# Feed-forward products by Strassen's algorithm, with streamed weights, behind an attention and Fourier kernel

## The chip, the cores and the metric

The kernel runs on one core of a Trainium2 chip. The metric is the device time of one execution in microseconds (us). Engines are named as the profile names them: PE is TensorE (PEld its weight loads), DVE is VectorE, ACT is ScalarE, POOL is GpSimd, SP is SyncE, which only issues DMAs; POOL issues DMAs too.

## The reference

```python
scores = np.matmul(q, k.transpose(0, 1, 3, 2)) / sqrt(64)   # q, k, v: 8 x 12 heads x 448 x 64
scores = np.einsum('bhij,hg->bgij', scores, w_pre)          # heads mixed
attn = softmax(scores)                                      # over the last axis
attn = np.einsum('bhij,hg->bgij', attn, w_post)             # heads mixed again
x = heads_side_by_side(attn @ v)                            # 8 x 448 x 768
u = x + np.real(fft(fft(x, axis=1), axis=2))
un = (u - mean(u)) / sqrt(var(u) + 1e-6)                    # over the last axis
out = u + np.maximum(un @ w_ch1, 0.0) @ w_ch2               # 768 -> 3072 -> 768
```

The two weights come as float64 and are used as fp32, as everything else is.

## The kernel before

It has two phases, and a scheduler that orders each engine's instructions. `u_scr`, `w1` and `w2` are tensors in DRAM that lead from the first phase to the second.

**The mix phase** (`mix_phase`) handles 8 batches of 45 tiles, each of 10 rows times 12 heads on the partitions. Per tile: a gather of scores `Kr` by an SP DMA, the head mixing on PE (L255, "mx", one call of two passes), the row maximum on DVE (L262, "nmx"), the exponential on ACT (L271, "PP"), the reciprocal of its sum on DVE (L279, L281, "rcp"), the mixing weights scaled by it on POOL (L284, "kw2s"), a product with them on PE (L292, "fl") and a copy to `Pav`. Beside the tiles stand the score products (L235), attention times v (L316), and the Fourier products (L346, L370) with the sum into `X` (L378 to L381), which SP stores to `u_scr`. POOL forms the folded halves `xo` and `xe` (L331, L333).

In the same phase the weights are converted: 96 pieces of 128 x 384. POOL loads the raw 64-bit words into one of two `raw` buffers (L398), DVE makes fp32 of them in seven operations (L409 to L422) on `tmp` and `top`, also in two buffers each, and SP stores `top` to `w1` or `w2` (L424). A piece is due every 3.5 tiles at the earliest, but the scheduler may take it sooner.

**The feed-forward phase** (`ffn_phase`) loads all weights into SBUF by 12 DMAs on POOL's queue (L538, L547) and takes 14 blocks of 256 tokens. SP loads `u` (L531). DVE and POOL normalise it, PE transposes it ("tp", L573), and ACT or DVE copies it to `ut`. The first product (L587, "hp") takes 24 column groups of six matmuls with 256 columns; a ReLU out of PSUM gives `h`. The second product (L601, "po") takes 192 matmuls with 384 columns a block, DVE adds it to `u` (L607), and SP stores the result (L609). A matmul in fp32 is two passes on PE, and the profile counts passes; a transpose is one.

Of the kernel before, what the change touches and what calls it, by code (L numbers as in the profile page):

```python
# [10 lines left out]
F32 = mybir.dt.float32  # L11
# [11 lines left out]
# Rows of a sequence are split as s = p * C + c and stand at c * PC + p.  # L23
# [3 lines left out]
# A mixing tile is R rows x NH heads on the partitions; a group is GT of them.  # L27
# [16 lines left out]
# Columns of a weight that are converted at a time, and mixing tiles between.  # L44
# [3 lines left out]
TB = 256  # L48
NTB = B * S // TB
NFC = DFF // P  # L50
NCC = DM // P
# [36 lines left out]
class _Evac:  # L88
    """Copies out of PSUM, shared between ScalarE and VectorE."""
# [34 lines left out]
def mix_phase(ctx, tc, ident, q, k, v, w_pre, w_post, u_scr, weights):  # L124
    """Talking-heads attention, its 2D Fourier transform and their sum, to u_scr.

    Beside it, the weights of `weights`, pairs of float64 bits and a float32 tensor."""
# [5 lines left out]
    praw = pool("praw", 3)  # L133
# [10 lines left out]
    pcv = pool("pcv", 2)  # L144
    cst = pool("cst")
# [193 lines left out]
    def emit_z(b, par, ch):  # L339
        """Along the sequence: Z[d, s'], d one chunk of the folded dimension."""  # L340
        d0, w = (EVEN, ODD)[par][ch]
        gs = groups[b * NG:(b + 1) * NG]
        ps = ms_tile()
        for g in gs:
            n = g["rows"]
            nc.tensor.matmul(ps[:w, :SH + 1], g["xf"][par][:n, d0:d0 + w],  # L346
                             ts[:n, g["gi"], par, :],
                             start=(g["gi"] == 0), stop=(g["gi"] == NG - 1))
        z = pzz.tile([w, S], F32, name=f"z{par}{ch}", tag=f"z{par}{ch}")
        batches[b]["z", par, ch] = z  # L350

        def done():
            rz, rp, hp = _row(z), _row(ps), PC // 2
            lo = _ap(z, 0, [[rz, w], [1, hp], [PC, C]])
            hi = _ap(z, hp, [[rz, w], [1, hp], [PC, C]])
            src = _ap(ps, 0, [[rp, w], [C, hp], [1, C]])
            mir = _ap(ps, SH, [[rp, w], [-C, hp], [-1, C]])
            ev.copy(lo, src, SH)
            (ev.negate if par else ev.copy)(hi, mir, SH)
        return 1, [done]  # L360

    def emit_s2(g):
        """Along the model dimension, and the sum with the attention's output."""
# [32 lines left out]
    def emit_convert(src, dst, r0, c0):  # L396
# [4 lines left out]
        lo, hi = raw[:, :, 0], raw[:, :, 1]  # L401
        top = pcv.tile([P, WC], F32, name="top", tag="top")
        tmp = pcv.tile([P, WC], F32, name="tmp", tag="tmp")
        topb, tmpb = top[:, :].bitcast(U32), tmp[:, :].bitcast(U32)

        def done():
            # The exponent is held within float32's: as float32s, the upper
            # words of 2^-127 and of the values right below 2^128.
# [3 lines left out]
            # Sign, exponent and the mantissa's upper 20 bits.  # L412
# [4 lines left out]
            # And its lower 32, as a multiple of the sign and the exponent.  # L417
# [4 lines left out]
            nc.vector.tensor_tensor(top[:, :], top[:, :], tmp[:, :], op=ALU.add)  # L422
# [12 lines left out]
    for gn, g in enumerate(groups):  # L435
# [19 lines left out]
        if g["gi"] == NG - 1:  # L455
# [7 lines left out]
    cuts = [(src, dst, r0, c0) for src, dst in weights  # L463
            for r0 in range(0, src.shape[0], P) for c0 in range(0, src.shape[1], WC)]
    for x, cut in enumerate(cuts):
# [34 lines left out]

@with_exitstack
def ffn_phase(ctx, tc, ident, u_scr, w_ch1, w_ch2, out):
    """Normalisation, the two products and the sum with u."""
# [6 lines left out]
    pw1 = pool("pw1")  # L510
    pw2 = pool("pw2")
    pu = pool("pu", 2)
    pun = pool("pun", 2)
    put = pool("put", 2)
    ph = pool("ph", NFC)
    pst = pool("pst", 4)
    ptp = pool("ptp", 2, space=bass.MemoryType.PSUM)
    pph = pool("pph", 3, space=bass.MemoryType.PSUM)
    ppo = pool("ppo", 3, space=bass.MemoryType.PSUM)

    ev = _Evac(nc)
    FW = 4
    NT2 = TB // P

    us, uts = {}, {}
# [3 lines left out]
    def load_u(t):  # L529
        us[t] = pu.tile([P, NT2, DM], F32, name="u", tag="u")  # L530
        nc.sync.dma_start(  # L531
# [3 lines left out]
    w1s, w2s = [], []  # L535
    for n in range(NFC // FW):
        w = pw1.tile([P, NCC, FW * P], F32, name=f"w1_{n}")
        nc.gpsimd.dma_start(  # L538
            out=w[:, :, :],
            in_=w_ch1[:, n * FW * P:(n + 1) * FW * P].rearrange(  # L540
                "(c p) f -> p c f", p=P))
        w1s.append(w)
        if n == 0:
            load_u(0)
    for n in range(NFC // FW):
        w = pw2.tile([P, FW, DM], F32, name=f"w2_{n}")
        nc.gpsimd.dma_start(  # L547
            out=w[:, :, :],
            in_=w_ch2[n * FW * P:(n + 1) * FW * P, :].rearrange(
                "(c p) d -> p c d", p=P))  # L550
        w2s.append(w)

    def norm(t):
        uts[t] = put.tile([P, NCC, TB], F32, name="ut", tag="ut")
        for x in range(NT2):
            u = us[t][:, x, :]
            st = pst.tile([P, 2, 6], F32, name="st", tag="st")
            for y in range(2):
                nc.vector.bn_stats(st[:, y, :], u[:, y * DH:(y + 1) * DH])
            mv = pst.tile([P, 2], F32, name="mv", tag="mv")  # L560
            nc.vector.bn_aggr(mv[:, :], st[:, :, :])
            rstd = pst.tile([P, 1], F32, name="rstd", tag="rstd")
            nc.vector.tensor_scalar(rstd[:, :], mv[:, 1:2], 1e-6, None, op0=ALU.add)  # L563
            nc.gpsimd.tensor_tensor(rstd[:, :], rstd[:, :], mhalf[:, :], op=ALU.pow)  # L564
            un = pun.tile([P, DM], F32, name="un", tag="un")
            nc.vector.tensor_scalar(un[:, :], u, mv[:, 0:1], rstd[:, :],
                                    op0=ALU.subtract, op1=ALU.mult)
            ev.d += 2400.0
            for y in range(2):
                ps = ptp.tile([P, 3, P], F32, name="tp", tag="tp")  # L570
                for c in range(3):
                    cc = 3 * y + c
                    nc.tensor.transpose(ps[:, c, :], un[:, cc * P:(cc + 1) * P],  # L573
                                        ident[:, :])
                ev.copy(uts[t][:, 3 * y:3 * y + 3, x * P:(x + 1) * P],
                        ps[:, :, :], 3 * P)

    norm(0)
    for t in range(NTB):
        if t + 1 < NTB:  # L580
            load_u(t + 1)
        ut = uts.pop(t)
        hs = []
        for fc in range(NFC):
            ps = pph.tile([P, TB], F32, name="hp", tag="hp")
            for c in range(NCC):
                nc.tensor.matmul(  # L587
                    ps[:, :],
                    w1s[fc // FW][:, c, (fc % FW) * P:(fc % FW + 1) * P],
                    ut[:, c, :], start=(c == 0), stop=(c == NCC - 1))  # L590
            h = ph.tile([P, TB], F32, name="h", tag="h")
            ev.relu(h[:, :], ps[:, :], TB)
            hs.append(h)
        if t + 1 < NTB:
            norm(t + 1)
        u = us.pop(t)
        for x in range(NT2):
            pss = [ppo.tile([P, DH], F32, name="po", tag="po") for _ in range(2)]
            for fc in range(NFC):
                for y in range(2):  # L600
                    nc.tensor.matmul(  # L601
                        pss[y][:, :], hs[fc][:, x * P:(x + 1) * P],
                        w2s[fc // FW][:, fc % FW, y * DH:(y + 1) * DH],
                        start=(fc == 0), stop=(fc == NFC - 1))
            for y in range(2):
                us_ = u[:, x, y * DH:(y + 1) * DH]
                nc.vector.tensor_tensor(us_, us_, pss[y][:, :], op=ALU.add)  # L607
                ev.d += 470.0
            nc.sync.dma_start(out=out[t * TB + x * P:t * TB + (x + 1) * P, :],  # L609
                              in_=u[:, x, :])  # L610
# [3 lines left out]
def kernel(  # L614
# [18 lines left out]
    w1 = scr.tile([DM, DFF], F32, name="w1")  # L633
    w2 = scr.tile([DFF, DM], F32, name="w2")
    mix_phase(tc, ident, q, k, v, w_pre, w_post, u_scr,
              [(moe_w_ch1, w1), (moe_w_ch2, w2)])
    ffn_phase(tc, ident, u_scr, w1, w2,
# [32 lines left out]
```

## Time and profile before

| | |
|---|---|
| median of 3 runs | 3351.37 us (3343.59 to 3355.14) |
| the profiled execution: span from first to last instruction | 3344.3 us |
| mean granted TensorE clock | 0.973 |
| PE busy | 3187.5 us (95%) |
| DVE, ACT, POOL busy | 872.3, 756.3, 464.3 us |
| moved by DMA | 223.49 MB |

For the profiled execution only the span is known; the time of a run also holds what lies around it. A row of a group gives the line, the engine, the operation, output and inputs, shapes and count, then busy time and mean ns of one, then the idle time just ahead of it and what ended it. The page's strips cut the span into 40 slices with a digit for tenths of busy time, and `PEclk` is the granted clock in tenths. A row of the windows gives the busy time of each engine in a stretch with the count of its instructions, then the granted clock, the share of the 16 DMA engines that was busy, and GB/s.

### The profile page before, as it was taken

The page shows a single profiled execution, that of the slowest core. Times are in us where ns is not written, and L with a number is a line of the kernel's source. Part 1 is how long each engine was busy: PE and PEld are TensorE (multiplying, and loading weights), DVE is VectorE, ACT ScalarE, POOL GpSimd, SP SyncE. Part 2 cuts the span into 40 slices and gives each one's busy share as a digit, 9 for nine tenths or more (in the row PEclk, how much of TensorE's full clock was granted, in tenths as well). Part 3 has the DMA queues.
Part 4 walks back from the last instruction along what each step waited for, and adds up shares of the span by engine and source line. Part 5 has one row for each costly group of instructions (what it writes and reads, how often), then busy time and mean ns, then how long its engine had stood idle before and what let it go on. Part 6 is the DMA issues. An engine that isn't in the chain of part 4 may idle for free.

```text
span 3344.3 us, 39975 instructions
## 1 busy us (share of the span) xinstructions
PE 3187.5 (95%) x15608; PEld 2291.8 (69%) x15608; DVE 872.3 (26%) x2367; ACT 756.3 (23%) x1842; POOL 464.3 (14%) x839
## 2 busy tenths in 40 slices
PE   6888878999999999996999999999999999999999
PEld 3555555767676767674876876876876876876876
DVE  4777766333333333333000000000000000000000
ACT  3332432545454545441000000000000000100000
POOL 4242331313131312111000000000000000000000
PEclk8998888999999999998999999999999999999999
DMA  7676665444444444446000000000000000000000
GB/s 191 155 182 171 164 175 145 105 86 98 84 99 83 101 82 85 79 96 237 1 19 10 10 19 10 10 19 10 10 19 10 10 19 10 10 19 10 10 10 10
DMA packets 98482, 223.49 MB, mean 67 GB/s; under 512 B 12671, under 2 KB 67967, under 8 KB 98295
## 3 DMA queue, kind: packets, MB, share of 16 engines
q1 hardware_dynamic: 73527, 131.26, 18.1%
q0 software_dynamic: 24768, 89.68, 9.3%
q8 instruction: 125, 2.05, 0.3%
q14 instruction: 62, 0.51, 0.0%
HBM read 102.91 MB, written 40.89 MB: 43 GB/s over the span
## 4 chain that ended last, share of the span: by engine, by line
PE 83%; DMA 9%; DVE 5%; issue 1%; POOL 1%; ACT 0%; SPq 0%; POOLq 0%; DVEq 0%; ACTq 0%
PE hp L587 26%; PE po L601 26%; PE fl L292 7%; PE ms L316 7%; DMA raw<-in_moe_w_ch_dram 6%; PE mx L255 6%; PE ms L235 4%; PE ms L370 4%; PE ms L346 2%; DMA w<-top 1%; PE ms L223 1%; DVE top L415 1%; DVE tmp L420 1%; PE tp L573 1%; DVE nmx L262 1%
## 5 line engine op out<-in xcount | busy, mean ns | idle before, releaser
L587 PE MATMUL hp<-ut,w 128*128 128x256 f32 x4032 | 873.1, 379 | 0.0
L601 PE MATMUL po<-w,h 128*128 128x384 f32 x2688 | 871.4, 486 | 0.0
L587 PEld LDWEIGHTS hp<-ut,w 128*128 128x128 f32 x4032 | 766.4, 190 | 107.3 <-ACT ut L106 0.3
L601 PEld LDWEIGHTS po<-w,h 128*128 128x128 f32 x2688 | 508.7, 190 | 349.0
L292 PEld LDWEIGHTS fl<-kw2s,PP 120*112 120x112 f32 (+1 forms) x2880 | 341.5, 181 | 205.9 <-issue 111.6
L118 ACT ACTIVATE h<-hp 128x256 f32<-128x256 f32 x238 | 91.2, 383 | 1556.6 <-PE hp L587 1556.6
L292 PE MATMUL fl<-kw2s,PP 120*112 120x120 f32 (+1 forms) x2880 | 381.5, 277 | 39.1 <-POOL kw2s L284 25.6
L255 PE MATMUL mx<-Kr,kw 120*120 120x448 f32 x720 | 348.1, 567 | 33.0 <-ACT PP L271 24.2
L271 ACT ACTIVATE PP<-mx,nmx 120x448 f32<-120x448 f32 x360 | 228.2, 634 | 470.9 <-DVE nmx L262 430.1
L316 PEld LDWEIGHTS ms<-vn,Pav 112*120 112x120 f32 (+1 forms) x3072 | 315.6, 182 | 18.2 <-issue 14.1
L316 PE MATMUL ms<-vn,Pav 112*120 112x64 f32 (+1 forms) x3072 | 314.8, 265 | 5.6 <-issue 4.7
L262 DVE TENSOR_REDUCE nmx<-mx 120x1 f32<-120x448 f32 x360 | 222.3, 617 | 234.1 <-PE mx L255 232.1
L607 DVE TENSOR_TENSOR u<-u,po 128x384 f32<-128x384 f32 x56 | 31.0, 554 | 872.5 <-PE po L601 870.0
L284 POOL TENSOR_SCALAR kw2s<-kw2g,rcp 120x120 f32<-120x120 f32 x360 | 145.8, 405 | 701.0 <-DVE rcp L281 615.0
L106 ACT COPY Pav<-fl 112x480 f32<-112x480 f32 x310 | 177.2, 572 | 252.7 <-PE ms L316 127.3
L564 POOL TENSOR_TENSOR rstd<-rstd,mhalf 128x1 f32<-128x1 f32 x28 | 15.7, 578 | 1522.2 <-DVE rstd L563 1522.2
L120 DVE TENSOR_SCALAR h<-hp 128x256 f32<-128x256 f32 x98 | 41.6, 425 | 669.3 <-PE hp L587 669.3
L235 PE MATMUL ms<-kT,qT 64*120 64x448 f32 (+1 forms) x768 | 207.8, 612 | 6.6 <-DVE Sb L108 5.1
L106 ACT COPY Sb<-ms 120x448 f32<-120x448 f32 (+1 forms) x324 | 161.1, 531 | 48.4 <-PE ms L235 48.2
L235 PEld LDWEIGHTS ms<-kT,qT 64*120 64x120 f32 (+1 forms) x768 | 57.1, 180 | 118.0 <-issue 69.3
L255 PEld LDWEIGHTS mx<-Kr,kw 120*120 120x120 f32 x720 | 108.0, 191 | 40.9 <-ACT PP L271 31.9
L279 DVE TENSOR_SCALAR rcp<-den 120x1 f32<-120x1 f32 x360 | 54.6, 152 | 214.1 <-ACT PP L271 208.4
(63 smaller groups left out, 1680.2 us busy)
## 6 DMA issues: line engine op xcount, KB each, us to landing
Kr<-Sb SPq DMA_DIRECT2D x352, 210.0 KB
raw<-in_moe_w_ch_dram POOLq DMA_DIRECT2D x96, 384.0 KB, 5.9
w<-top SPq DMA_DIRECT2D x96, 192.0 KB
w<-w POOLq DMA_DIRECT2D x12, 1536.0 KB, 13.2
rawq<-in_q_dram POOLq DMA_DIRECT2D x96, 112.0 KB, 6.2
rawk<-in_k_dram POOLq DMA_DIRECT2D x96, 112.0 KB, 6.4
vn<-in_v_dram POOLq DMA_DIRECT2D x48, 224.0 KB, 4.8
u<-u_scr SPq DMA_DIRECT2D x14, 768.0 KB
```

The costliest lines, as they stand in the source:

```text
L106: self.nc.scalar.copy(out=out, in_=in_)
L118: self.nc.scalar.activation(out, in_, ACTF.Relu)
L235: nc.tensor.matmul(sp[:n, :S], st["qT", hp][x * D:(x + 1) * D, g["i0"]:g["i0"] + n], st["kT", hp][x * D:(x + 1) * D, :], start=True, stop= ...
L255: nc.tensor.matmul(mx[:m, :S], kw1[:m, :m], tiles[T]["Kr"][:m, :], start=True, stop=True)
L262: nc.vector.tensor_reduce(nmx[:m, :], tiles[T]["mx"][:m, :S], axis=AX.X, op=ALU.max, negate=True)
L271: nc.scalar.activation(PP[:m, :], tiles[T]["mx"][:m, :S], ACTF.Exp, bias=tiles[T]["nmx"][:m, :], accum_out=den[:m, :])
L284: nc.gpsimd.tensor_scalar(kw2s[:m, :], kw2g[:m, :], rcp[:m, :], 1.0, op0=ALU.mult, op1=ALU.mult)
L292: nc.tensor.matmul(fl[:PC, jc * KR:(jc + 1) * KR], tiles[T]["PP"][:m, jc * PC:(jc + 1) * PC], tiles[T]["kw2s"][:m, :], start=True, stop=True)
L316: nc.tensor.matmul(ps[:n, hl * D:(hl + 1) * D], g["Pav"][:, jc * NH + h, :n], st["v", h // 2][:, h % 2, jc * D:(jc + 1) * D], start=(jc == ...
L370: nc.tensor.matmul(ps[:n, :DH + 1], st["z", par, ch][:, i0:i0 + n], tab[:w, ch, :], start=(ch == 0), stop=(ch == len(chunks) - 1))
L587: nc.tensor.matmul(ps[:, :], w1s[fc // FW][:, c, (fc % FW) * P:(fc % FW + 1) * P], ut[:, c, :], start=(c == 0), stop=(c == NCC - 1))
L601: nc.tensor.matmul(pss[y][:, :], hs[fc][:, x * P:(x + 1) * P], w2s[fc // FW][:, fc % FW, y * DH:(y + 1) * DH], start=(fc == 0), stop=(fc = ...
```

## The change

Each feed-forward product is split into 2 x 2 blocks and done in seven block products instead of eight, with sums of blocks on both sides (Winograd's form of Strassen's algorithm). A block of tokens is 512 instead of 256, so there are seven.

- The mix phase forms the sums of weight blocks. Four converted pieces, one from each quarter of a weight, make a unit in one buffer `wu` of eight slots; POOL adds four sums (L431), and SP stores seven slots to `w1s` (three DMAs a unit, runs of 512 bytes) or `w2s` (one DMA). There are 24 units and one buffer. Raw q and k have two buffers instead of three.
- The feed-forward phase keeps no weights. Per 512 tokens SP streams 12 tiles of `w1s` (1344 KB each, three buffers, L589) and 14 of `w2s` (1152 KB each, four buffers, L594).
- The first product takes the column groups in pairs, 42 matmuls of 256 columns a pair, in six pairs. The seven products go into three PSUM banks per group, some on top of others, and each is copied or added to `h` by ACT or DVE before the next goes on top. DVE forms the ReLUs and the sums of `h`.
- The second product takes 168 matmuls of 384 columns per 512 tokens. The next block's normalisation stands between its products.
- `u` is loaded and the result stored by POOL, one DMA of 1536 KB each.

```diff
-TB = 256
+TB = 512
...
-    praw = pool("praw", 3)
+    praw = pool("praw", 2)
...
+    pwu = pool("pwu")
...
+            if key not in units:
+                units[key] = [pwu.tile([P, 8, WC], F32, name="wu", tag="wu"), 0]
...
-            nc.sync.dma_start(out=dst[r0:r0 + P, c0:c0 + WC], in_=top[:, :])
+            if units[key][1] == 4:
+                for out, x, op, y in sums:
+                    nc.gpsimd.tensor_tensor(wu[:, out, :], wu[:, x, :], wu[:, y, :],
+                                            op=op)
+                store(units.pop(key)[0])
...
+            def store(wu, n=n, kc=kc):
+                for j in range(WC // P):
+                    nc.sync.dma_start(out=w1s[n * (WC // P) + j, :, :, kc, :],
+                                      in_=wu[:, 0:7, j * P:(j + 1) * P])
...
+    pw1 = pool("pw1", 3)
+    pw2 = pool("pw2", 4)
...
+    def first(t):
+        ub = ubs.pop(t)
+        h = ph.tile([P, 5, NM, HT], F32, name="h", tag="h")
+        h11, h12, h22, h21, hs1 = (h[:, x] for x in range(5))
+        for m0 in range(0, NM, 2):
+            ms = range(m0, m0 + 2)
+            w = {m: load_w1(m) for m in ms}
+            ps = {}
+            for i in ORDER:
+                for m in ms:
+                    key = {0: "P", 5: "P", 6: "P", 3: "P", 1: "Q"}.get(i, "R")
+                    opens = i in (0, 1, 4)
+                    if opens:
+                        ps[key, m] = ps_tile()
+                    p = ps[key, m][:, :HT]
+                    for kc in range(NK):
+                        nc.tensor.matmul(p, w[m][:, i, kc, :], ub[:, i, kc, :],
+                                         start=opens and kc == 0, stop=kc == NK - 1,
+                                         skip_group_check=True)
+                    if i == 0:
+                        nc.scalar.copy(out=h11[:, m, :], in_=p)
...
+                    elif i == 5:
+                        nc.scalar.copy(out=h21[:, m, :], in_=p)
...
+                    elif i == 6:
+                        nc.vector.tensor_tensor(h22[:, m, :], h22[:, m, :], p, op=ALU.add)
+                    else:
+                        nc.scalar.activation(h12[:, m, :], p, ACTF.Relu)
...
+    def second(t, h):
...
+        for n, i in enumerate(ORDER):
...
+            for half in range(2):
+                w = load_w2(i, half)
+                for x in range(NT2 // 2):
...
+                    for kf in range(NQ):
+                        nc.tensor.matmul(
+                            p, lhs[i][:, half * NQ + kf, x * P:(x + 1) * P], w[:, kf, :],
...
+            if 1 <= n <= NT2 and t + 1 < NTB:
+                norm(t + 1, n - 1)
```

Three places where the scheduler's order differs. On PE, in the first product, before: one bank ("hp") after another, six matmuls each, with weights `w1_0` that stay.

```order
L587 MATMUL hp_13670<-ut_13627,w1_0_13601 128x256 x6
L587 MATMUL hp_13679<-ut_13627,w1_0_13601 128x256 x6
L587 MATMUL hp_13688<-ut_13627,w1_0_13601 128x256 x6
L587 MATMUL hp_13697<-ut_13627,w1_0_13601 128x256 x6
L587 MATMUL hp_13706<-ut_13627,w1_1_13605 128x256 x6
```

On PE, the same place now: one pair of the first block. `w1t_13878` is its first tile (A), `w1t_13880` its second (B), and a `ps` is a PSUM bank.

```order
L647 MATMUL ps_13882<-ub_13577,w1t_13878 128x256 x9
L647 MATMUL ps_13887<-ub_13577,w1t_13880 128x256 x3
L647 MATMUL ps_13892<-ub_13577,w1t_13878 128x256 x3
L647 MATMUL ps_13897<-ub_13577,w1t_13880 128x256 x3
L647 MATMUL ps_13902<-ub_13577,w1t_13878 128x256 x3
L647 MATMUL ps_13907<-ub_13577,w1t_13880 128x256 x3
L647 MATMUL ps_13887<-ub_13577,w1t_13880 128x256 x3
L647 MATMUL ps_13902<-ub_13577,w1t_13878 128x256 x3
L647 MATMUL ps_13907<-ub_13577,w1t_13880 128x256 x3
L647 MATMUL ps_13887<-ub_13577,w1t_13880 128x256 x3
L647 MATMUL ps_13882<-ub_13577,w1t_13878 128x256 x3
L647 MATMUL ps_13887<-ub_13577,w1t_13880 128x256 x3
```

The scheduler has drawn three of A's products (0, 5 and 6, on one bank, with a copy by ACT after each of the first two) ahead of the first use of B. Tile B takes the buffer that the pair before gives free with its row before last. All pairs but the first of each block look like this.

On DVE, between two conversions, before: `top_3512` belongs to one piece and `top_3671` to the next.

```order
L409 TENSOR_SCALAR tmp_3672<-raw64_3669 128x384
L418 TENSOR_SCALAR tmp_3513<-top_3512 128x384
L410 TENSOR_SCALAR tmp_3672<-tmp_3672 128x384
L262 TENSOR_REDUCE nmx_1490<-mx_1480 120x1
L108 COPY qT_1497<-ms_1498 128x448
L420 SCALAR_TENSOR_TENSOR tmp_3513<-raw64_3510,tmp_3513 128x384
L108 COPY Sb_1344<-ms_1509 120x448
L279 TENSOR_SCALAR rcp_1566<-den_1523 120x1
L422 TENSOR_TENSOR top_3512<-top_3512,tmp_3513 128x384
L281 RECIPROCAL rcp_1566<-rcp_1566 120x1
L413 TENSOR_SCALAR top_3671<-tmp_3672 128x384
```

On DVE now, from the end of one unit (L427, the last operation of its fourth piece) to the first write of the next one's `wu` (L418).

```order
L427 TENSOR_TENSOR wu_8143<-wu_8143,tmp_8522 128x384
L415 TENSOR_SCALAR tmp_8628<-tmp_8628 128x384
L261 TENSOR_REDUCE nmx_4094<-mx_4078 120x1
L278 TENSOR_SCALAR rcp_4201<-den_4162 120x1
L280 RECIPROCAL rcp_4201<-rcp_4201 120x1
L414 TENSOR_SCALAR tmp_8785<-raw64_8762 128x384
L415 TENSOR_SCALAR tmp_8785<-tmp_8785 128x384
L418 TENSOR_SCALAR wu_8627<-tmp_8628 128x384
L261 TENSOR_REDUCE nmx_4173<-mx_4159 120x1
L420 SCALAR_TENSOR_TENSOR wu_8627<-raw64_8608,wu_8627 128x384
```

The first write to the new `wu` waits for the old one's sums and stores, and stands a few rows behind them in DVE's order, with the tiles' operations behind it. The last conversion stands after the 156th of 360 row maxima in this order, before after the 112th.

On SP, at the seam of the phases, before: the last batch's stores to `u_scr`, and the first loads of `u` behind them.

```order
L390 DMA u_scr<-X 112x768
L390 DMA u_scr<-X 8x768
L390 DMA u_scr<-X 104x768
L390 DMA u_scr<-X 16x768
L390 DMA u_scr<-X 96x768
L390 DMA u_scr<-X 24x768
L390 DMA u_scr<-X 88x768
L531 DMA u<-u_scr 128x2x768 x2
```

On SP now, the same place.

```order
L589 DMA w1t<-w1s 128x2688 x3
L594 DMA w2t<-w2s 128x2304 x4
L389 DMA u_scr<-X 112x768
L389 DMA u_scr<-X 8x768
L389 DMA u_scr<-X 104x768
```

Seven weight tiles stand ahead of those stores; the first two loads of `u` are on POOL's queue, ahead of that phase's last operations there.

More of the change, by code (lines that the diff above doesn't have):

```diff
@@ L46 @@
 WSTEP = 3.5
-TB = 256
+TB = 512
 NTB = B * S // TB
-NFC = DFF // P
-NCC = DM // P
 def _consts():
@@ L393, in emit_s2, with emit_convert @@
         return 2, [done]
-    def emit_convert(src, dst, r0, c0):
+    units = {}
+    def emit_convert(key, slot, src, r0, c0, sums, store):
         raw = pcv.tile([P, WC, 2], U32, name="raw64", tag="raw64")
@@ L462, in mix_phase @@
                 due(f + n + 7.6 + x, lambda g=groups[gn - NG + 1 + x]: emit_s2(g))
-    cuts = [(src, dst, r0, c0) for src, dst in weights
-            for r0 in range(0, src.shape[0], P) for c0 in range(0, src.shape[1], WC)]
-    for x, cut in enumerate(cuts):
+    for x, cut in enumerate(weights(nc)):
         due(x * WSTEP, lambda cut=cut: emit_convert(*cut))
@@ L545, in ffn_phase @@
[L545 to L576, printed above, removed]
@@ L579, in ffn_phase @@
+    load_u(0)
+    for x in range(NT2):
+        norm(0, x)
     for t in range(NTB):
@@ L581, in ffn_phase @@
             load_u(t + 1)
[L582 to L610, printed above, removed]
+        second(t, first(t))
 @with_exitstack
```

154 lines of the change are left out of this document (123 added, 31 removed).

## The prediction

> **What bounds the kernel now.** The page comes first: TensorE (PE) is busy 95% of the span, but unevenly.
>
> ```profile
> span 3344.3 us, 39975 instructions
> PE   6888878999999999996999999999999999999999
> PEclk8998888999999999998999999999999999999999
> ```
>
> The first seven slices (580 us) are the exception: 8 tenths busy at a clock of 0.8 to 0.9. The rest is full but for one slice at the seam. The groups, kept apart by shape, name the two big products; a matmul call in fp32 is two passes, so 4032 passes are 2016 calls.
>
> ```profile
> L587 PE MATMUL hp<-ut,w 128*128 128x256 f32 x4032 | 873.1, 379 | 0.0
> L601 PE MATMUL po<-w,h 128*128 128x384 f32 x2688 | 871.4, 486 | 0.0
> ```
>
> Neither ever waits. The chain of waits from 1500 us on (start, duration, what) shows the seam and then matmuls back to back:
>
> ```profile
> 1534.69 18.18 PE ms L370 x56
> 1552.96 0.55 DVE X L378
> 1554.97 8.01 DMA u_scr<-X
> 1563.63 15.47 DMA u<-u_scr
> 1582.21 3.01 PE tp L573 x12
> 1585.22 62.85 PE hp L587 x288
> 1648.07 0.66 PE tp L573 x6
> 1650.02 61.28 PE po L601 x190
> 1711.30 62.16 PE hp L587 x288
> ```
>
> So a 256-column call costs 62.16 / 144 = 0.4317 us, a 384-column call 61.28 / 95 = 0.645 us, a transpose 0.11 us. From 1553 to 3344.3, 1791.3 us, TensorE's count of matmuls sets the time, plus a seam of 29 us in which it waits for the u load behind the weights.
>
> Ahead of 1553 the limits differ. The busy times cut at the last conversion (PE, PEld, DVE, ACT, POOL with counts, clock, DMA share, GB/s), and the premix matmul L255 alone over the same stretches:
>
> ```profile
> 0.00:603.50 603.50, 482.49 (x2597) 318.44 (x2598) 409.82 (x1105) 198.95 (x481) 202.81 (x341) 0.88 0.66 166
> 603.50:1553.00 949.50, 947.11 (x6124) 678.34 (x6124) 336.42 (x966) 442.45 (x1068) 241.22 (x464) 1.00 0.46 95
> 0.00:603.50 603.50, 120.52 (x224) 36.66 (x224) 0.88 0.66 166
> 603.50:1553.00 949.50, 227.61 (x496) 71.34 (x496) 1.00 0.46 95
> DVE tmp L409 <- DMA raw<-in_moe_w_ch_dram: 129.1, 61, 5.5
> ```
>
> L255 is two passes per mixing tile: 112 tiles up to 603.5 us, then 248 tiles at 3.83 us each with TensorE full. While weights are converted a tile takes over 5 us, because VectorE (DVE), which every tile needs, waits in its queue for raw weights (last row, from the list of waits: us, times, the longest).
>
> **The feed-forward part.** The order has 252 matmuls of 256 columns and 168 of 384 per 512 tokens, against 288 and 192 before. Seven blocks at the old pace: 7 x 252 x 0.4317 = 761.5 us and 7 x 168 x 0.645 = 758.5 us. Transposes stay 24 per 512 tokens: 6 x 24 x 0.11 = 15.8 us, the first block's being in the seam.
>
> New are waits inside a pair. Tile A's first product, its copy, its second product, its copy and its third stand in a row on TensorE. What a copy by ScalarE (ACT) costs between two matmuls:
>
> ```profile
> 1644.66 3.40 PE L587 MATMUL hp<-ut,w 128*128 128x256 f32 x15
> 1648.10 0.38 ACT L118 ACTIVATE h<-hp 128x256 f32<-128x256 f32 x1 [4.80 <-PE hp L587]
> 1583.14 0.48 ACT L106 COPY ut<-tp 128x384 f32<-128x384 f32 x1 [47.88 <-PE tp L573]
> 1583.67 1.14 PEld L573 LDWEIGHTS tp<-ident,un 128*128 128x128 f32 x6 [0.33 <-ACT ut L106]
> ```
>
> A pass is modelled to end 379 - 216 = 163 ns after the next could start; ACT starts 0.04 us after that end (1648.06 to 1648.10), takes 0.38, and the weight load follows 0.05 us behind (1583.62 to 1583.67); I add 0.11 until the matmul. So 0.75 us, twice in each of 5 pairs of 7 blocks: 70 x 0.75 = 52.5 us. The other copies stand behind other products.
>
> Tile B's load (1344 KB) starts when the pair before is through with its A, and B is needed 4 groups of three and two of those waits later: 4 x 1.295 + 1.5 = 6.7 us. The nearest load is that of u, 768 KB, alone on the SP queue; the DMA engines' rate is that of a full stretch:
>
> ```profile
> 1839.70 0.38 SPq L531 DMA_DIRECT2D u<-u_scr  x1
> 1844.00 1.48 DVE L559 BATCH_NORM_STATS2 st<-u 128x6 f32<-128x384 f32 x3 [6.71 <-DMA u<-u_scr]
> 1575.00:1580.00 5.00, 0.00 (x0) 0.00 (x0) 1.54 (x6) 0.00 (x0) 1.10 (x2) 0.50 1.02 401
> ```
>
> 4.3 us for 786 kB, and 590 kB more at 401 GB/s: 5.8 us, 0.9 us before need. I take no wait. If the load queued 1.3 us behind it shares the engines evenly, it lands after 7.9 us, 1.2 us late. The second product needs 1152 KB per 12 x 0.645 = 7.7 us with four buffers, 152 GB/s of 401: hidden. VectorE gets 11 operations of 256 or 512 columns for a pair; at
>
> ```profile
> L607 DVE TENSOR_TENSOR u<-u,po 128x384 f32<-128x384 f32 x56 | 31.0, 554 | 872.5 <-PE po L601 870.0
> rawq<-in_q_dram POOLq DMA_DIRECT2D x96, 112.0 KB, 6.2
> ```
>
> that is at most 11 x 0.554 x 512 / 384 = 8.1 us beside 42 x 0.4317 = 18.1 us of matmuls: hidden, and without that cover 42 pairs x 8.1 = 341 us. Two buffers for raw q and k in place of three cost nothing: a head pair comes every two tiles, 7.7 us, so a load of 6.2 us (second row) has 15.
>
> The seam: u and the first seven weight tiles are now issued ahead of the last u_scr stores, so the 24 us of landing go. What is late next is VectorE's work on the last X (2.0 us, 1552.96 to 1554.97), then half of the transposes (3.0 us, the x12 row): 5.0 us, and the cold clock costs 2.0 us as before. h may also wait for the u_scr stores, at most 4 us more. The end: one 1536 KB store from the POOL queue for two small ones from SP:
>
> ```profile
> 3340.74 0.33 SPq L609 DMA_DIRECT2D out_dram<-u  x1
> ```
>
> 3.6 us to the span's end now; then 0.6 for the sum, 0.9 to issue, and 4.3 + 787 kB at 401 = 6.3: 7.8 us. Together 5.0 + 2.0 + 761.5 + 758.5 + 15.8 + 52.5 + 7.8 = 1603.1 against 1791.3: **188.2 us less**.
>
> **The conversions.** The same 96, but in 24 units of four, with one buffer wu for a unit, four sums on GpSimd (POOL) and 1344 KB of stores for 768 KB. VectorE may not write the next unit before the stores have landed, and the order puts that write few instructions on; behind it in VectorE's queue stand the maxima and reciprocals of every tile, so ACT, POOL and PE wait as well. Rows for one unit: all operations on tmp and L415 (96 conversions), a POOL sum of the same width, two stores of 192 KB (chain), and the DMA engines near full:
>
> ```profile
> 0.00:610.00 610.00, 245.56 (x576) 0.88 0.66 166
> L415 DVE SCALAR_TENSOR_TENSOR top<-raw,top 128x384 uint32<-128x384 uint32 x96 | 56.4, 587 | 1.9
> 212.27 0.99 POOL L333 TENSOR_TENSOR xo<-X 120x383 f32<-120x383 f32 x1
> 212.30 2.33 DVE L415 SCALAR_TENSOR_TENSOR top<-raw,top 128x384 uint32<-128x384 uint32 x1
> 213.22 0.98 POOL L331 TENSOR_TENSOR xe<-X 120x383 f32<-120x383 f32 x1
> 217.13 6.43 DMA w<-top
> 224.60 6.95 DMA w<-top
> 25.00:30.00 5.00, 5.00 (x30) 2.44 (x28) 2.62 (x5) 2.20 (x5) 1.17 (x2) 0.87 1.03 267
> ```
>
> A conversion is (245.6 + 56.4) / 96 = 3.15 us. A unit: four conversions, less the first steps of two that can run ahead, 11; VectorE's tile work between, 3 tiles at 336.4 / 248 = 1.36, 4; raw loads, as now 129.1 / 96 = 1.34 each, 5.4 at most, I take 2.6. Sums 4 x 0.99 and some 1.2 of other POOL work in between: 5.2. Store: 6.4 for the first 192 KB, the other 1.18 MB at 267 GB/s 4.4: 10.8. In all 33.6, say 34 us. It starts near 29 us: 29 + 24 x 34 - 11 = 834 us. By then the order has passed 156 tiles; 204 x 3.83 = 781. The mix ends at 1615, **62 us later**. From below: TensorE alone needs 156 x 3.83 = 597 us for those tiles, 25 a unit; from above, 512-byte runs of the w1 stores at half that rate, sums between other POOL work: 44.
>
> Sum: 3344.3 + 62 - 188.2 = 3218 us of span; the median stands 7.1 us above the profiled span, so **3225 us**.
>
> Row 212.30 shows a further price: VectorE's operation took 2.33 us instead of 0.587 while two POOL operations ran. The Trainium skill, SBUF — State Buffer, section "Who interferes with whom", says why: a VectorE instruction with two SBUF inputs and a GpSimd instruction take one shared port pair in turn, the later fully blocked. The row agrees. In my sum the blocked time falls into VectorE's wait for the store; by the rule alone every sum that meets VectorE's work would add its length.
>
> **The rivals.**
> *The unit ring decides (slower).* With sums and stores at 44 us a unit, 24 x 10 = 240 us more: 3465. It loses from 39.2 us a unit, that is (188.2 - 62) / 24 = 5.3 above mine. For: one buffer, in-order VectorE; against: two raw tiles wait loaded. 0.16.
> *Conversions hide.* Spread over 156 tiles instead of 112, they leave TensorE near full: 27 us a unit, 168 less: 3057. For: a tile's 3.83 us on TensorE stand against 96 x 3.15 / 156 + 1.36 = 3.3 on VectorE; against: 129.1 us of waits even with double buffers. 0.12.
> *POOL's sums block VectorE on the path* for their whole length, as in row 212.30: 96 x 0.99 = 95 more, 3320. 0.10.
> *Tile B late:* 35 x 1.2 = 42, 3267. 0.07.
> *Late, and the clock falls.* Granted clock at 0.5 us steps around the seam:
>
> ```profile
> 1555.00:1555.50 0.50, 0.00 (x0) 0.96 0.10 12
> 1555.50:1556.00 0.50, 0.00 (x0) 0.50 0.52 209
> 1586.00:1586.50 0.50, 0.50 (x3) 0.82 0.00 0
> ```
>
> The last matmul ended at 1552.9; 2.6 us later the clock halved, and 4 us after the restart at 1582.2 it was back: 2.0 us lost each time. A load 3.5 us late would cost 35 x 5.5 = 193: 3418. 0.03. The Trainium skill, TensorE: Matmul & The Clock Gate, "HAM oscillation — how this bites in real kernels", allows idle gaps up to about 3.4 us; by that even this case would lose only near the limit. The row's 2.6 us decides.
> That the change doesn't do what it says is excluded by the counts.
>
> **How the numbers follow.** Forecast 0.52, the rivals 0.48. Its own range, units of 30 to 38 us, is 3130 to 3320. To leave out no more than 2 in 10 I go from 3100 (28.8 us a unit) to 3385 (40.7); what lies beyond is most of the ring's and half of the hidden case. A measurement of this kernel tells about 0.3% (10 us) from no change. Slower are the ring and the clock, 0.19, less 0.02 that ends near the start; the same 0.04, that and as much from the blocked and late cases; faster the rest, 0.79.
>
> **What would show it.** Right: 3528 passes of L647 and 2352 of L687 at 62.16 / 288 and 61.28 / 190 us; the first L647 some 5 us behind the last L369; PE idle 0.75 us twice a pair for ACT; the last conversion near 820 us; L418 waiting for stores. Wrong: conversions over before 700 us or after 950; PE waiting on w1t loads; clock below 1.00 in the last half.

## The result and the profile after

The changed kernel takes 3274.77 us (median of 4 runs, 3265.39 to 3282.36), the kernel before 3347.48 beside it: a ratio of 0.9773, with a 95% interval of 0.9747 to 0.9800. It is faster by some 73 us. The forecast was 3225 us, 126 less than the median then shown. Direction and range held; the gain is 58% of what was forecast.

The page of the changed kernel, its span and the strips for PE and the granted clock:

```profile
span 3274.6 us, 39030 instructions
PE   6878888888899999999999999999999999999998
PEclk8898799999999999999999999999999999999999
```

PE is below 9 tenths for the first eleven slices now, 900 us, and in the last; before, it was for the first seven and at the seam. The groups of the two products, then the stages (PE, PEld, DVE, ACT, POOL busy with counts, clock, DMA share, GB/s), cut at the last conversion and at the end of the mix, and the premix matmul L254 alone over the first two:

```profile
L647 PE MATMUL ps<-ub,w1t 128*128 128x256 f32 x3528 | 791.0, 384 | 50.8 <-DVE h L661 17.2
L687 PE MATMUL ps<-w2t,h 128*128 128x384 f32 x2352 | 763.6, 486 | 0.0
```

```profile
0.00:830.00 830.00, 667.57 (x3694) 446.80 (x3695) 471.52 (x1276) 281.77 (x680) 348.44 (x517) 0.90 0.61 155
830.00:1646.20 816.20, 790.08 (x5031) 562.68 (x5030) 287.87 (x825) 362.07 (x868) 202.15 (x386) 0.99 0.45 97
1646.20:3274.60 1628.40, 1567.17 (x6048) 1133.30 (x6046) 387.90 (x744) 150.15 (x392) 22.33 (x34) 0.99 0.40 149
...
0.00:830.00 830.00, 162.44 (x314) 50.27 (x315) 0.90 0.61 155
830.00:1646.20 816.20, 188.25 (x406) 59.24 (x406) 0.99 0.45 97
```

Both counts are as announced, 3528 and 2352. The mix ends at 1646.2 us instead of 1553, 93 us later; the rest takes 1628.4 us instead of 1791.3, 163 us less. Up to the last conversion 157 tiles pass (314 passes), then 203 in 816.2 us, 4.02 us each and not 3.83. What stands still is in the list of waits (engine, line, who released it: us, times, the longest):

```profile
DVE tmp L414 <- DMA raw<-in_moe_w_ch_dram: 155.3, 71, 6.3
DVE wu L418 <- DMA w1s<-wu: 68.1, 11, 9.5
DVE wu L418 <- DMA w2s<-wu: 32.8, 9, 7.2
...
PE ms L222 <- DMA rawq<-in_q_dram: 28.9, 14, 9.7
PE ms L222 <- DMA rawk<-in_k_dram: 19.5, 11, 2.9
PE ps L647 <- DVE h L661: 17.2, 5, 4.4
PE ps L647 <- ACT h L651: 16.2, 35, 0.5
...
PE ps L647 <- DMA w1t<-w1s: 1.2, 1, 1.2
```

The raw loads cost DVE 155.3 us (129.1 before), the stores of a unit 101 us (12.8 us on L413 before). The waits of PE for L661 are new, and those for raw q and k are 48.4 us in all. Before, they were 9.7, nearly all of it one wait:

```profile
PE ms L223 <- DMA rawq<-in_q_dram: 9.5, 2, 9.4
```

**The seam.** The timeline of PE between the phases: the last L369 ends at 1646.1, the first L647 begins at 1650.58, 4.5 us later.

```profile
1644.01 2.11 PE L369 MATMUL ms<-tdo,z 128*88 128x385 f32 x6
...
1648.15 1.53 PE L620 MATMUL ps<-ident,un 128*128 128x128 f32 x12 [1.38 <-DVE X L380]
...
1650.58 19.59 PE L647 MATMUL ps<-ub,w1t 128*128 128x256 f32 x90
1670.64 1.56 PE L647 MATMUL ps<-ub,w1t 128*128 128x256 f32 x6 [0.46 <-ACT h L651]
1672.66 17.10 PE L647 MATMUL ps<-ub,w1t 128*128 128x256 f32 x78 [0.46 <-ACT h L657]
1690.22 1.56 PE L647 MATMUL ps<-ub,w1t 128*128 128x256 f32 x6 [0.46 <-ACT h L651]
```

The lower rows are a steady pair: PE stops twice for a copy by ACT. From 1670.64 to 1690.22 a pair takes 19.58 us; 84 passes at 62.16 / 288 are 18.13. So a stop costs 0.73 us, though only 0.46 is shown as idle, since the end of the pass before it is modelled late.

**Between blocks.** The timeline of all engines where block 1 goes over into block 2 (start, duration, what; in brackets the idle time ahead and its releaser):

```profile
1878.70 0.81 POOL L707 DMA_DIRECT2D out_dram<-u  x1 [227.13 <-DVE u L696]
...
1888.14 0.77 POOL L583 DMA_DIRECT2D u<-u_scr  x1 [8.63 <-DMA out_dram<-u]
...
1895.30 1.02 DVE L607 BATCH_NORM_STATS2 st<-u 128x6 f32<-128x384 f32 x2 [3.55 <-DMA u<-u_scr]
1896.24 0.41 DVE L661 TENSOR_TENSOR h<-h,ps 128x256 f32<-128x256 f32 x1
...
1896.70 4.15 PE L647 MATMUL ps<-ub,w1t 128*128 128x256 f32 x18 [3.35 <-DVE h L661]
```

This is a chain of five: POOL stores the result; the load of the next `u` goes into the same buffer, so it is issued only when the store has landed; DVE has the statistics of that `u` in its queue ahead of the sum L661 of the first pair, and stands before them for 3.55 us; PE's next product goes on top of the bank that L661 reads. The blocks begin at 1650.58, 1877.65, 2108.33, 2339.80, 2574.64, 2807.28 and 3041.10: the first takes 227.07 us, the next five 3.6, 4.4, 7.8, 5.6 and 6.8 more, 28.1 us in all.

**The end.** The last pass of L687 is over at 3265.7, 8.9 us before the span's end; in between stands the one large store.

### The profile page after: what moved, and what is told of

The parts are those of the page before. It is cut to its first block, busy times and chain, and to the rows that moved or that the text cites. A ratio compares the mean times of both kernels' runs of the same rounds, so it can differ in the third digit from the quotient of the medians.

```text
span 3274.6 us, 39030 instructions
## 1 busy us (share of the span) xinstructions
PE 3024.8 (92%) x14768; PEld 2142.8 (65%) x14768; DVE 1147.3 (35%) x2843; ACT 794.0 (24%) x1940; POOL 572.9 (17%) x937
## 4 chain that ended last, share of the span: by engine, by line
PE 49%; issue 29%; DMA 13%; DVE 5%; POOL 2%; ACT 1%; SPq 1%; POOLq 0%; DVEq 0%; ACTq 0%
PE ps L687 10%; PE ms L315 9%; PE ps L647 9%; PE fl L291 6%; DMA raw<-in_moe_w_ch_dram 6%; PE mx L254 5%; PE ms L369 3%; PE ms L234 3%; PE ms L345 2%; DMA w1s<-wu 2%; DMA rawk<-in_k_dram 2%; DMA out_dram<-u 1%; DMA u<-u_scr 1%; DVE nmx L261 1%; DMA w2s<-wu 1%
## 5 line engine op out<-in xcount | busy, mean ns | idle before, releaser
L647 PE MATMUL ps<-ub,w1t 128*128 128x256 f32 x3528 | 791.0, 384 | 50.8 <-DVE h L661 17.2
L647 PEld LDWEIGHTS ps<-ub,w1t 128*128 128x128 f32 x3528 | 669.6, 192 | 172.2 <-ACT h L651 30.2
L687 PE MATMUL ps<-w2t,h 128*128 128x384 f32 x2352 | 763.6, 486 | 0.0
L687 PEld LDWEIGHTS ps<-w2t,h 128*128 128x128 f32 x2352 | 445.0, 190 | 303.8
L291 PEld LDWEIGHTS fl<-kw2s,PP 120*112 120x112 f32 (+1 forms) x2880 | 350.4, 185 | 241.6 <-issue 117.2
L291 PE MATMUL fl<-kw2s,PP 120*112 120x120 f32 (+1 forms) x2880 | 392.3, 282 | 66.9 <-POOL kw2s L283 56.3
L254 PE MATMUL mx<-Kr,kw 120*120 120x448 f32 x720 | 350.7, 571 | 21.9 <-ACT PP L270 16.2
L283 POOL TENSOR_SCALAR kw2s<-kw2g,rcp 120x120 f32<-120x120 f32 x360 | 155.5, 432 | 691.1 <-DVE rcp L280 622.4
L696 DVE TENSOR_TENSOR u<-u,ps 128x384 f32<-128x384 f32 x98 | 54.4, 555 | 551.9 <-PE ps L687 551.9
L653 DVE TENSOR_TENSOR h<-h,ps 128x256 f32<-128x256 f32 x84 | 35.4, 422 | 332.9 <-PE ps L647 332.9
L622 ACT COPY ub<-ps 128x384 f32<-128x384 f32 x56 | 24.0, 483 | 479.8 <-PE ps L620 479.7
L254 PEld LDWEIGHTS mx<-Kr,kw 120*120 120x120 f32 x720 | 109.5, 193 | 30.0 <-ACT PP L270 20.8
```

The costliest lines, as they stand in the source:

```text
L254: nc.tensor.matmul(mx[:m, :S], kw1[:m, :m], tiles[T]["Kr"][:m, :], start=True, stop=True)
L283: nc.gpsimd.tensor_scalar(kw2s[:m, :], kw2g[:m, :], rcp[:m, :], 1.0, op0=ALU.mult, op1=ALU.mult)
L291: nc.tensor.matmul(fl[:PC, jc * KR:(jc + 1) * KR], tiles[T]["PP"][:m, jc * PC:(jc + 1) * PC], tiles[T]["kw2s"][:m, :], start=True, stop=True)
L647: nc.tensor.matmul(p, w[m][:, i, kc, :], ub[:, i, kc, :], start=opens and kc == 0, stop=kc == NK - 1, skip_group_check=True)
L687: nc.tensor.matmul(p, lhs[i][:, half * NQ + kf, x * P:(x + 1) * P], w[:, kf, :], start=opens and half == 0 and kf == 0, stop=half == 1 and ...
```

## The experiments

The theory from this trace: the conversions cost what DVE's waits in its queue cost; with two buffers the raw q and k come late; the late `u` load and the ACT copies stand on PE's path. Each experiment takes out one of these. Ratios are to the kernel before, run beside them, with 95% intervals.

### Three buffers for raw q and k (praw3)

```diff
-    praw = pool("praw", 2)
+    praw = pool("praw", 3)
...
-    s1 = [(4, 7, ALU.add, 3), (5, 4, ALU.subtract, 0),
-          (6, 0, ALU.subtract, 7), (2, 1, ALU.subtract, 5)]
+    s1 = [(4, 2, ALU.add, 3), (5, 4, ALU.subtract, 0),
+          (6, 0, ALU.subtract, 2), (2, 1, ALU.subtract, 5)]
```

The unit's buffer has seven slots here instead of eight, which makes the room, and the constant `kw2` stands in the buffers of `kw2s`.

> The changed kernel with three buffers for raw q and k again (room for them: the unit tile has seven blocks instead of eight, the block that is only an input of two sums standing where the last sum is written). Theory: after the last conversion 203 mixing tiles took 816.2 us, 4.02 us each, against 3.83 before, because TensorE waits for raw q and k and the clock falls in those waits. With three buffers the 203 tiles cost 777, so the mix ends near 1607 instead of 1646 and the kernel takes about 3236 us (39 less). Rival: the slower tiles come from something else that the change brought (sums still on POOL, other order), and the waits for q and k only show it; then 3265 to 3285 us.

Measured: 3256.79 us, ratio 0.9748 (0.9704 to 0.9791), which can't be told from the change's own 0.9773. By windows, cut at its last conversion:

```profile
0.00:869.00 869.00, 169.01 (x314) 51.51 (x314) 0.84 0.59 149
869.00:1660.00 791.00, 187.85 (x406) 58.89 (x406) 1.00 0.46 99
```

The mix ended at 1654.9 here. The 203 tiles after the conversions took 786 us, 3.87 each: there the theory holds, 30 of 39 us. But the stretch before took 869 us instead of 830, at a clock of 0.84. The profiled execution was the longest of the four (3283.18; the others 3248.98 to 3258.33), so how much of this increase belongs to the edit is open.

### Two buffers alone, in the kernel before (before_praw2)

```diff
-    praw = pool("praw", 3)
+    praw = pool("praw", 2)
```

> The kernel before with one edit of the change alone: two buffers for raw q and k in place of three. The prediction said that this costs nothing. Theory now: TensorE waits for raw q and k as in the changed kernel, where 203 tiles took 39 us more (0.19 us a tile); over the 248 tiles after the conversions 47 us, so about 3394 us, with PE ms waiting for rawq and rawk in the list of waits. Rival: the loads came late only behind what the change put on POOL and the DMA engines; then 3335 to 3360 us.

Measured: 3368.43 us, ratio 1.0063 (1.0042 to 1.0083), 21 us slower. PE's waits and the premix by windows:

```profile
PE ms L223 <- DMA rawq<-in_q_dram: 23.7, 11, 9.4
...
PE ms L223 <- DMA rawk<-in_k_dram: 20.2, 14, 3.6
```

```profile
0.00:603.50 603.50, 119.39 (x229) 36.78 (x230) 0.89 0.66 167
603.50:1579.00 975.50, 226.92 (x492) 71.54 (x490) 0.99 0.45 93
```

By 603.5 us 114.5 tiles have passed; the other 245.5 take until the mix ends at 1589.8, 4.02 us each as in the changed kernel. The mix is 37 us longer. 16 us come back at the seam, where the span from the last L370 to the first L587 is 15.7 us instead of some 32: the `u` load lands in 7.1 us instead of 15.5. The weight load last issued ahead of it went out 24 us earlier here, and 7 us earlier before. So the two buffers cost by themselves, without the rest of the change.

### Four buffers for the weight tiles of the first product (w4)

```diff
-    pw1 = pool("pw1", 3)
-    pw2 = pool("pw2", 4)
+    pw1 = pool("pw1", 4)
+    pw2 = pool("pw2", 3)
```

> The changed kernel with four buffers for the first product's weight tiles and three for the second's. Tiles A and B are then both there when a pair starts, and the products alternate 0A 0B 5A 5B. Theory: the copies of ScalarE hide behind the other tile's product; 70 gaps of 0.73 us go, 51 us less, about 3224 us; the second product's loads stay hidden with three buffers. Rival: TensorE then runs ahead of the loads and waits for weights once a pair (1 us or more, 42 pairs), or for the second product's third buffer: 3265 us or more.

Measured: 3226.39 us, ratio 0.9650 (0.9630 to 0.9671), 48 us less than the change. In the first block the first product runs through on PE's timeline without a stop (the last 493 of its 504 passes). The waits for weight tiles that the rival foresaw don't occur; the five waits for L661 stay, 17.2 us. The timeline of the first block:

```profile
1649.77 106.57 PE L647 MATMUL ps<-ub,w1t 128*128 128x256 f32 x493
```

### The normalisation queued later on DVE (normlate)

```diff
+            last = nc.vector.tensor_tensor(h21[:, s, :], h11[:, s, :], h21[:, s, :],
+                                           op=ALU.subtract)
+        return h, last.ins
...
+                with tc.issue_after(last):
+                    norm(t + 1, n - 1)
```

> The changed kernel with one thing tied: the normalisation of the next 512 tokens is queued on VectorE behind the last VectorE instruction of the first product, so its wait for the u load no longer stands ahead of the sums of the first pair of tiles. Theory: five waits of TensorE of 2.5 to 4.5 us and the clock lost behind them go; blocks two to six took 230.7 to 234.8 us against 227.1 for the first, 28 us in all, so about 3247 us. Rival: TensorE there waits for the products' own chain (third product behind the sum), and VectorE's stall only shows it: 3265 to 3285 us.

Measured: 3248.45 us, ratio 0.9707 (0.9673 to 0.9742), 26 us less. The place that waited 3.35 us runs through now, and each of the first six blocks takes 227.07 us, as only the first did:

```profile
1883.40 19.59 PE L647 MATMUL ps<-ub,w1t 128*128 128x256 f32 x90
```

### The conversions spread over the tiles (spread)

```diff
+        with after("pool"):
+            nc.gpsimd.dma_start(
+                out=raws[x].rearrange("p n w -> p (n w)"),
+                in_=src[r0:r0 + P, c0:c0 + WC].bitcast(U32))
...
         def done():
+          with after("dve"):
...
-        due(x * WSTEP, lambda cut=cut: emit_convert(*cut))
+        due(x // 4 * 4 * WSTEP + (x % 4 - 1) * CSTEP, lambda x=x, cut=cut: emit_raw(x, *cut[2:5]))
+        due(x // 4 * 4 * WSTEP + x % 4 * CSTEP, lambda x=x, cut=cut: emit_convert(x, *cut))
```

`after` queues what follows behind the last kw2s on POOL or the last maximum on DVE; CSTEP is 2.5. So the four conversions of a unit stand 2.5 tiles apart, and its sums and stores have the rest of its 14 tiles.

> The changed kernel with the conversions tied to the mixing tiles: each unit of four is spread over 14 tiles, a raw load is issued on POOL behind the kw2s of a tile two and a half tiles ahead of its conversion, and the conversion stands on VectorE behind the maximum of its tile. The same work, 96 conversions, 96 sums, 48 stores. Theory: what the conversions cost is VectorE standing in its queue for loads and stores that have not landed, not the work; then the mix is bound by TensorE's 3.83 us a tile, 360 of them from about 29 us, 1408 us, plus up to 70 us of waits for raw q and k: the mix ends at 1410 to 1480 instead of 1646 and the kernel takes 3036 to 3109 us. Rival: the conversions cost what they cost wherever they stand (VectorE's work, its port shared with POOL's sums, DMA engines near full): 3230 to 3290 us.

Measured: 3093.24 us, ratio 0.9255 (0.9222 to 0.9287), 182 us less than the change with the same work. The mix ends at 1460 us; it and DVE's wait for raw weights, 9.8 us where it was 155.3 (stores 1.7 where it was 101):

```profile
0.00:1460.00 1460.00, 1388.50 (x8720) 974.46 (x8721) 759.40 (x2098) 645.67 (x1549) 527.00 (x903) 0.98 0.59 142
```

```profile
DVE tmp L427 <- DMA raw<-in_moe_w_ch_dram: 9.8, 9, 2.2
```

DVE is busy for 759.4 us there, as in the two mix stages of the change together (471.5 + 287.9); only the waits are gone. The edit spaces the conversions and also ties them to places in the queues; no run takes these two apart.

### The same spreading in the kernel before (before_spread)

The same edit, one conversion each 3.5 tiles.

> The kernel before, with its 96 conversions tied to the mixing tiles in the same way, one each 3.5 tiles. It asks how much of the changed kernel's gain by spreading belongs to the change at all. Theory: up to the last conversion 112 tiles took 603.5 us where TensorE alone would need 29 + 112 x 3.83 = 458; these 145 us were VectorE's waits, and they go: the mix ends near 1410 instead of 1553, about 3202 us. Rival: before, with two buffers and no sums, the waits were mostly beside TensorE's work and the clock was the loss: 3300 us or more.

Measured: 3192.49 us, ratio 0.9543 (0.9527 to 0.9559), 155 us less. The mix ends at 1406 us:

```profile
0.00:1406.00 1406.00, 1369.98 (x8720) 968.92 (x8720) 747.47 (x2069) 642.27 (x1548) 438.34 (x804) 0.99 0.58 136
```

So the greater part of what spreading gains was there to be had before the change.

### Spread, with three buffers for raw q and k (spread_p3)

Both edits together.

> The changed kernel with the conversions spread over the tiles and three buffers for raw q and k. Theory: with the conversions off the path, the waits for q and k (42.4 us) and the clock lost behind them are all that holds the mix above 1408 us; they go, the mix ends near 1410 instead of 1460, and the kernel takes about 3043 us. Rival: three buffers gain 18 us, as they did where the conversions were not spread: 3075 us.

Measured: 3054.72 us, ratio 0.9133 (0.9105 to 0.9161), 38.5 us less than spread alone. PE's waits for q and k fall from 42.4 to 14 us:

```profile
PE ms L224 <- DMA rawq<-in_q_dram: 9.7, 2, 9.5
...
PE ms L224 <- DMA rawk<-in_k_dram: 4.3, 4, 1.7
```

Neither number of the expectation was met, and it lies nearer to the theory's (50) than to the rival's (18).

### The sums on DVE (sums_dve)

```diff
-                    nc.gpsimd.tensor_tensor(wu[:, out, :], wu[:, x, :], wu[:, y, :],
+                    nc.vector.tensor_tensor(wu[:, out, :], wu[:, x, :], wu[:, y, :],
```

> The changed kernel with the 96 sums of the weight blocks on VectorE instead of POOL. A unit took 33.3 us (first store to last, 766.5 us for 23). Theory of the prediction: the sums lie in a unit's chain between its last conversion and its store, 5.2 us on POOL; on VectorE four of 0.555 us, 2.2; a unit takes 30.4, the mix ends 24 x 2.9 = 70 us sooner, about 3205 us. Rival: POOL's sums run beside VectorE's waits for raw loads, which are what sets the unit; then VectorE only gains 96 x 0.555 = 53 us of work in a stretch where the tiles need it: 3275 to 3330 us.

Measured: 3261.98 us, ratio 0.9742 (0.9703 to 0.9780): 13 us less, with overlapping intervals. Its first and last store of a unit on SP's timeline, and DVE's waits:

```profile
68.27 1.77 SPq L532 DMA_DIRECT2D w1s<-wu  x1
...
835.17 0.39 SPq L543 DMA_DIRECT2D w2s<-wu  x1
```

```profile
DVE tmp L414 <- DMA raw<-in_moe_w_ch_dram: 141.8, 61, 5.9
...
DVE wu L418 <- DMA w1s<-wu: 44.4, 9, 10.3
...
DVE wu L418 <- DMA w2s<-wu: 14.7, 9, 4.6
```

A unit takes 766.9 / 23 = 33.3 us as before. The sums are 54 us of work on DVE, its conversions take 21 us less (298.8 instead of 319.7), and it waits 55 us less for loads and stores; two more stops ahead of L418, 14.7 us, have no releaser in the list. So moving the sums doesn't shorten a unit, and the theory's 70 us don't come. The rival doesn't hold either: 163 tiles pass by the last conversion, at 831 us, instead of 157, and what the stretch takes beyond TensorE's need falls from 200 to 178 us (worked out under the next run).

### One tile for each block of a unit (slots)

```diff
-                units[key] = [pwu.tile([P, 8, WC], F32, name="wu", tag="wu"), 0]
+                units[key] = [{}, 0]
...
+            wu[slot] = slot_tile(slot)
+            top = wu[slot][:, :]
...
+            for i in range(7):
+                nc.sync.dma_start(out=w2s[i, kf // NQ, :, kf % NQ, :], in_=wu[i][:, :])
```

> The changed kernel with the unit tile of eight blocks as eight tiles of one block each in the same bytes, each stored by itself (168 stores of 192 KB instead of 48 of 448 and 1344): VectorE may write a block of the next unit as soon as the last sum has read that block and its own store has landed. With the sums on VectorE a unit still took 33.3 us; so either the stores' landing or the raw loads set it. In the changed kernel VectorE waits 101 us for stores and 155 us for raw loads, and the conversions' stretch holds 200 us more than TensorE needs for its tiles, 55 more than before. Theory: those 55 are the waits for stores; they mostly go, the mix ends 40 to 55 us sooner, 3220 to 3235 us. Rival: the raw loads set the pace, the waits for stores are filled by longer waits for raw loads: 3255 to 3290 us, with VectorE's wait for raw above 200 us.

Measured: 3259.77 us, ratio 0.9749 (0.9724 to 0.9775), 15 us less, with overlapping intervals. The premix by windows, cut at the last conversion, and DVE's wait for raw weights:

```profile
0.00:638.50 638.50, 128.49 (x230) 39.17 (x230) 0.87 0.71 179
638.50:1626.40 987.90, 227.33 (x492) 71.46 (x490) 0.99 0.45 94
```

```profile
DVE tmp L418 <- DMA raw<-in_moe_w_ch_dram: 139.1, 67, 5.7
```

The waits for stores are gone from DVE's list (in their place it waits 14.1 us for POOL's sums), the conversions end at 638.5 us instead of 830, four of them in 25 us instead of 33, and the mix ends only 20 us sooner. So the wait for a unit's store did set the pace of the conversions, but that pace is not the price, as far as two traces tell whose times differ by little more than the runs of one kernel do. The order lets 115 tiles pass beside them instead of 157. What the stretch takes beyond TensorE's need for its tiles (29 us to start, 3.83 a tile) goes from 830 - 29 - 157 x 3.83 = 200 us to 638.5 - 29 - 115 x 3.83 = 169. By this count 31 of the 101 us of waits had reached the end, and 8 of these are lost again because 42 more tiles come later at 4.03 us. Both readings had a part wrong: the theory its size, the rival the growth of the raw waits.

### All four together (best)

The edits of spread, praw3, w4 and normlate.

> All four together: spread conversions, three buffers for raw q and k, four and three buffers for the weight tiles, the normalisation tied behind the first product. Theory: the parts stand in different stretches and add up: 3093 - 50 (q and k) - 51 (gaps for copies, two in each of 35 pairs) - 28 (block seams) = 2964 us; TensorE is then the bound from 29 us to the end: 1379 + 7 x 219.8 us and the seam. Rival: without the gaps the weight loads come late and give back up to half of it: 3000 us or more.

Measured: 2968.53 us, ratio 0.8873 (0.8847 to 0.8899). Its two phases by windows:

```profile
0.00:1421.00 1421.00, 1372.39 (x8731) 969.10 (x8732) 759.24 (x2091) 643.31 (x1552) 526.29 (x901) 1.00 0.60 146
1421.00:2968.20 1547.20, 1537.77 (x6039) 1135.01 (x6037) 391.55 (x752) 148.76 (x389) 22.33 (x36) 1.00 0.43 157
```

PE is busy 98% of the span at full clock, and each of the first six blocks takes 219.77 us (they begin at 1422.89, 1642.66, 1862.43 and so on), against 219.8 from the counts (252 x 0.4317 + 168 x 0.645 + 24 x 0.11). The sum of the expectation is met within 5 us. With the gains as measured one at a time (182, 38.5, 48 and 26 us) it would be 2980, 12 us more than measured. It beats the kernel before with its conversions spread (3192.49 us) by 224 us.

## Why the prediction was right, and where it was not

Its own sum beside what the profile shows:

| stretch | predicted | measured |
|---|---|---|
| to the last conversion (tiles passed) | 834 (156) | 830 (157) |
| the other tiles, to the mix's end | 781 | 816.2 |
| seam, cold clock with it | 5.0 + 2.0 | 4.4 |
| seven blocks: matmuls, transposes, stops for ACT | 1588.3 | 1615.1 |
| tail | 7.8 | 8.9 |
| span | 3218 | 3274.6 |

The span missed by 56 us, and two steps carry it. The median was put 7.1 us above the span and lies 0.2 above it.

**The counts and the pace** held: the seven block products take what 7/8 of the old ones should. best shows it with nothing in the way.

**The stops for ACT**, taken at 0.75 us, are 0.73; w4 takes them out and gains 48 of 51 us. **The w1t loads** kept up: one wait of 1.2 us in 84 loads. The seam and the tail held within 3 us; the cold clock did not come: PE waits 1.4 us there and not 29, and the granted clock stayed at 1.00.

**"Two buffers for raw q and k in place of three cost nothing: a head pair comes every two tiles, 7.7 us" failed.** The transposes of q and k on PE's timeline between two batches:

```profile
1216.07 0.60 PE L222 MATMUL ms<-ident,rawq 112*128 112x112 f32 x4
...
1220.04 0.55 PE L222 MATMUL ms<-ident,rawq 112*128 112x112 f32 x4
...
1225.07 0.57 PE L222 MATMUL ms<-ident,rawq 112*128 112x112 f32 x4 [1.40 <-DMA rawq<-in_q_dram]
1228.34 0.98 PE L222 MATMUL ms<-ident,rawk 112*128 112x112 f32 x4 [2.69 <-DMA rawk<-in_k_dram]
```

A pair comes every 4 us, one tile, so that with two buffers a load has 8 us less its time in POOL's queue, and it takes 6.0. The mean over a batch hid the burst. praw3, before_praw2 and spread_p3 show it from three sides: 30 us in the tiles after the conversions, 37 us in the mix before the change, 38.5 us once the conversions are out of the way. In the changed kernel itself the edit's whole price was not settled.

**A wait that the sum did not have: the `u` load behind the result's store.** The prediction saw that both are now one POOL DMA each, and costed that at the tail alone. It did not follow the two buffers of `u`, nor what stands behind the statistics in DVE's queue. 28.1 us; normlate moves the statistics and gains 26.

**The conversions: the right sum from wrong parts.** 34 us a unit were forecast, 33.3 measured. But the prediction had the sums in the chain with 5.2 us, and with sums_dve, where they are shorter, a unit takes 33.3 us still; the raw loads, taken at 2.6 us a unit, stop DVE for 155.3 / 24 = 6.5. The wait for the store is real (slots), 101 / 24 = 4.2 us. Against the old 145 us beyond TensorE's need, the stretch has 200: 55 us, where 62 were forecast for the whole mix.

**The rivals.** POOL's sums lengthen DVE's work, but not by the rival's 95 us: the seven conversion operations took 319.7 us in all, against 312.7 before and 298.8 with the sums off POOL (sums_dve). That is 21 us for 96 sums, and a unit takes as long without it. That the conversions could hide was put at 3057 us, and spread reaches 3093 with them spread over the whole phase; in the change's own order they did not. What would show the forecast wrong included a clock below 1.00 in the last half: it is 0.99, but from the waits for `u` and not for weights.

## What to carry to other kernels

An in-order engine that stands before a load or a store makes everything queued behind it late: look at what stands behind the waiting instruction, and tie work that has slack behind the instruction it may follow (182 us here, without one operation less). Check a buffer count against the shortest distance between two uses, not the mean. A pace that a trace confirms is no price: ask how much of each wait reaches the end.

## What the runs showed of the hardware

A pause of PE of much the same length may or may not cost the clock. After the block seam shown above, whose pause ends at 1896.70, by windows; then after the next one, on PE's timeline and by windows of PE alone (busy, clock, DMA share, GB/s):

```profile
1898.00:1899.00 1.00, 1.00 (x7) 0.87 (x6) 0.93 (x3) 0.38 (x1) 0.40 (x1) 1.00 0.00 0
```

```profile
2126.49 5.84 PE L647 MATMUL ps<-ub,w1t 128*128 128x256 f32 x18 [2.46 <-DVE h L661]
```

```profile
2127.50:2130.50 3.00, 3.00 (x8) 0.50 0.34 72
```

After 3.35 us of pause the clock stayed at 1.00 and 18 passes took 4.15 us; after 2.46 us it was 0.50 for over 3 us, from a moment at which PE was working again, and 18 passes took 5.84. So the length alone doesn't tell, and neither the 2.6 us nor the 3.4 us of the prediction is a limit below which the clock is safe: 2.46 us was enough here. The Trainium skill, TensorE: Matmul & The Clock Gate, section "What's actually happening", has activity judged in windows that run on by themselves; these two seams agree with that, though no run shows the windows themselves.
